# Opening of an attention and feed-forward kernel: weights in pairs, one more row from split parts, new orders on three engines

## The chip, the cores and the metric

The kernel runs on one core of one Trainium2 chip. Its engines are TensorE (PE; its weight loads are PEld), VectorE (DVE), ScalarE (ACT), GpSimd (POOL) and SyncE (SP), which issues the DMAs. The metric is the device time of one execution in microseconds (us), as the median of several runs.

## The reference

For 8 batches and 8 heads, x (512 tokens by 64) and a state (32 rows by 64) attend to each other; the 544 rows of a batch then pass through a feed-forward network of 512 to 2048 to 512.

```python
scores = scale * x @ state.T            # softmax over the 32 state rows
xread  = softmax(scores) @ state
scores2 = scale * state @ x.T           # softmax over the 512 tokens
sread  = softmax(scores2) @ x
rows = concat([xread, sread], axis=2)   # heads side by side: (8 * 544, 512)
h = rows @ w_in                         # 512 x 2048
g = h - tanh(h)
out = g @ w_out                         # 2048 x 512, float32
```

## The kernel before

The work goes in chunks: chunk i < 8 holds the 512 tokens of batch i, chunk 8 the 256 state rows of all batches. Instead of xread @ w_in, the kernel multiplies the attention weights a (tokens by 256 of head and state row) with m = state @ w_in, which it makes for each batch. A chunk takes 16 steps f, one for each 128 columns of the hidden layer: products into a PSUM bank (`hps`), tanh on ScalarE, the subtraction on VectorE, then the output products with row block f of w_out, summed over f in four banks. Operands are split into a high and a low part (a cast on ScalarE, a subtraction on VectorE), and three products (high x high, high x low, low x high) replace one in full precision. In the opening some products still take unsplit float32 operands; each such product is two instructions in the trace.

The weights come as 64-bit floats, 512 KB for each block of 128 rows or columns, and are turned into 32 bits by four steps: a shift on VectorE, a conversion of the low word on ScalarE, a carry on VectorE, an integer addition on VectorE.

**The opening** (steps 0 to 7 of chunk 0 and the hidden parts of steps 0 and 1 of chunk 1) is written out by hand as three lists, `lines`, one each for PE, DVE and ACT. Each engine runs its list strictly in that order. An entry is a letter and a number:

- a, r, b, p: the four steps (shift, conversion, carry, addition) of block j of w_in; p stores the block to `wf`. u, w, v, y: the same for block f of w_out; after y more loads are issued (`REFILL`). i, l: high and low part of that block.
- S, c, T, U: scores, their copy, their transposition. M, B, E, Z, I, J, N, A: maximum, subtraction, exp, sum, epsilon, reciprocal, scaling, transposition back: the first softmax, number 0 and 1 for batch 0, 2 and 3 for batch 1.
- m: block j of m for batches 0 and 1 (up to j = 3 for two batches more), from PE; k, R: copies to where PE reads it. e: more of them (j = 0, 1) for four batches. s, t, f, n: copies of e and m into tiles `e` and `f` that are stored to DRAM (`mearly`, `mlast`).
- P, d: high and low part of batch 0's attention; j, x: high and low part of block f of m (`fine`), for f of 4 and more. K, C: the same for batch 1.
- h, H: first and second half of the hidden products of step n (8 and 9 are chunk 1). X: tanh. L: subtraction. G, g: high and low part of the result, tile `g`. O, Q: output products for tokens 0 to 255 and 256 to 511. V: halves of chunk 0's output to DRAM.

`ops` and `more` state what each entry must follow. For f below `WHOLE_ROWS` the output products take the unsplit block and result. A tile belongs to a tag with a fixed count of buffers, and a new tile waits until all uses of the tile before it in that buffer are over. Tag `g` has three (`GB`), and the opening's tenants are in turn `head` (inputs of the first scores), the tiles e0 and e1, then the results g. DMAs are issued in order from SP's queue. All after the opening is ordered by a planner from estimates.

At the end, chunk 8 merges its three products: one matmul of 512 columns against the high weights gives high x high and high x low side by side in one bank, one of 256 adds low x high, and a copy on ScalarE (L480) and an addition on VectorE (L481) bring the halves together ahead of the tanh (L483).

Of the kernel before, what the change touches and what calls it, by code (L numbers as in the profile page):

```python
# [45 lines left out]
def attention_ffn(ctx: ExitStack, tc: tile.TileContext, early, xT, xn, bh, sm, sl, win, wout, xout, sout):  # L46
# [32 lines left out]
    wo = [cpool.tile([P, 2, DM], F32R, name=f"wo{f}") for f in range(NFF // 2)]  # L79
# [23 lines left out]
    def slots(name, shape, dtype):  # L103
        return pool.tile(shape, dtype, tag="slots", name=name, bufs=NFF // 2)
# [52 lines left out]


# [518 lines left out]
    def turn(j):  # L677
        es[j] = pool.tile([P, 512], F32, tag="e", name=f"e{j // 2}{j % 2}")
# [8 lines left out]
    def maximum(j):  # L687
        ms[j] = pool.tile([P, 16, 1], F32, tag="m1", name=f"m1{j // 2}{j % 2}")
        nc.vector.reduce_max(ms[j], e3(j), axis=AX.X)

    def sub_max(j):
        nc.vector.tensor_sub(e3(j), e3(j), ms[j].broadcast_to([P, 16, 32]))

    def exp(j):
        nc.scalar.activation(es[j], es[j], AF.Exp, scale=SCALE)

    def sums(j):
        if j < 2:
# [1 line left out]
        elif j == 2:  # L700
            z1.append(pool.tile([P, 2, 16, 1], F32, tag="z1", name="z1", bufs=1))
        if j > 1:
            zs[j] = z1[0][:, j - 2]
        nc.vector.reduce_sum(zs[j], e3(j), axis=AX.X)
# [9 lines left out]
    def normalize(j):  # L714
        nc.vector.tensor_mul(e3(j), e3(j), zs[j].broadcast_to([P, 16, 32]))
# [10 lines left out]
    def win_step(n):  # L726
        def run(j):
            if j not in csteps:
# [3 lines left out]
                csteps[j] = wcols[j].steps(wb[j // 2][:, j % 2], "cr")  # L732
            csteps[j][n]()
            if n == 3:
                nc.sync.dma_start(rows(wf[j // 4], j), wb[j // 2][:, j % 2].rearrange("p (r f) -> p r f", r=4))
        return run

    def wout_step(n):
        def run(f):
            if f not in wsteps:  # L740
                if f < WHOLE_ROWS:
                    if f % 2 == 0:
                        whole.append(pool.tile([P, 2, 512], F32, tag=("mr", "stage")[f // 2], name=f"wor{f}", bufs=(RRB, SB)[f // 2]))
                    worows[f] = whole[f // 2][:, f % 2]
                else:
                    worows[f] = pool.tile([P, 512], F32, tag="wor", name=f"wor{f}", bufs=RB)
                wsteps[f] = wos[f].steps(worows[f], "s")
            wsteps[f][n]()
            if n == 3:
                with ExitStack() as gates:  # L750
                    for x in stores:
                        gates.enter_context(tc.issue_after(x))
                    load(int(f in REFILL))
        return run

# [333 lines left out]
```

## Time and profile before

| | |
|---|---|
| median of 3 runs | 640.68 us (640.53 to 641.02) |
| profiled execution, its own time | 641.04 us |
| its span, first to last instruction | 639.3 us |
| PE busy | 631.6 us (99%), 3766 instructions |
| DVE busy | 440.0 us (69%) |
| ACT busy | 354.8 us (56%) |
| granted TensorE clock | 1.0 throughout |

Busy time is the sum of an engine's instructions. Since matmuls are pipelined and their ends are modelled, a row of a matmul may reach beyond the start of the next; the distance of starts is its cost in a stream. "idle before" in a row is the time that the engine stood still ahead of it, with what released it.

### The profile page before, as it was taken

What the parts mean: (1) busy time and instruction counts of PE and PEld (TensorE: products, weight loads), DVE (VectorE), ACT (ScalarE), POOL (GpSimd) and SP (SyncE); (2) the same over time, 40 slices, a digit from 0 to 9 for tenths busy, and PEclk for the clock granted to TensorE, in tenths of its full rate; (3) what the DMA queues carried; (4) which work ended last, traced back from release to release, by engine and by line L of the source; (5) the groups of instructions that cost most, each with busy time, mean ns of one, the idle gap of its engine ahead of it and who ended that gap; (6) DMA issues with size and microseconds to landing.
All of it is one profiled execution on the core that took longest, in us unless ns stands there. A gap on an engine that the chain in (4) does not pass through costs nothing.

```text
span 639.3 us, 10152 instructions
## 1 busy us (share of the span) xinstructions
PE 631.6 (99%) x3766; PEld 501.0 (78%) x3766; DVE 440.0 (69%) x775; ACT 354.8 (56%) x650; POOL 0.3 (0%) x5
## 2 busy tenths in 40 slices
PE   7999999999999999999999999999999999999997
PEld 4466866888888788878888788878888788888886
DVE  5999997798683874688563678396664875454663
ACT  4876677687783444656553458264543453343553
POOL 0000000000000000000000000000000000000000
PEclk9999999999999999999999999999999999999999
DMA  8994897477885335644533236772463024221410
GB/s 322 402 319 142 298 319 262 149 233 215 255 270 148 104 98 201 173 135 127 174 115 104 79 111 208 246 271 94 122 197 91 34 91 141 77 65 34 131 34 33
DMA packets 66592, 105.84 MB, mean 166 GB/s; under 512 B 12272, under 2 KB 32368, under 8 KB 66544
## 3 DMA queue, kind: packets, MB, share of 16 engines
q1 hardware_dynamic: 66544, 105.21, 50.7%
q8 instruction: 29, 0.48, 0.3%
q14 instruction: 19, 0.16, 0.1%
HBM read 69.01 MB, written 35.65 MB: 164 GB/s over the span
## 4 chain that ended last, share of the span: by engine, by line
PE 91%; DVE 5%; DMA 2%; ACT 1%; issue 0%; SPq 0%
PE ops L522 19%; PE ops L524 18%; PE ops L523 18%; PE hps L470 8%; PE hps L472 8%; PE hps L471 8%; PE hps L455 2%; PE mps L216 2%; PE rps L402 1%; PE hps L456 1%; DMA w00d<-in_win 1%; PE mps L215 1%; PE sps L284 1%; PE mps L766 1%; DVE w L150 1%; PE hps L828 1%
## 5 line engine op out<-in xcount | busy, mean ns | idle before, releaser
L522 PE MATMUL ops<-wo,g 128*128 128x512 f32 x534 | 209.3, 394 | 0.3 <-ACT g L116 0.3
L523 PE MATMUL ops<-wo,g 128*128 128x512 f32 x534 | 208.2, 390 | 0.0
L524 PE MATMUL ops<-wo,g 128*128 128x512 f32 x534 | 198.4, 390 | 0.0
L483 ACT ACTIVATE t<-hps 128x512 f32<-128x512 f32 x118 | 70.4, 598 | 148.4 <-PE hps L472 145.6
L483 DVE TENSOR_TENSOR t<-hps,t 128x512 f32<-128x512 f32 x118 | 81.0, 687 | 103.5 <-ACT t L483 103.2
L522 PEld LDWEIGHTS ops<-wo,g 128*128 128x128 f32 x534 | 100.3, 188 | 27.0 <-issue 3.0
L524 PEld LDWEIGHTS ops<-wo,g 128*128 128x128 f32 x534 | 100.0, 188 | 23.0 <-issue 1.7
L523 PEld LDWEIGHTS ops<-wo,g 128*128 128x128 f32 x534 | 100.3, 188 | 21.6 <-issue 1.6
L117 DVE TENSOR_TENSOR g<-t,g 128x512 fp32r<-128x512 f32 (+1 forms) x134 | 87.4, 656 | 32.7 <-ACT g L116 32.1
L116 ACT CAST g<-t 128x512 fp32r<-128x512 f32 (+1 forms) x134 | 79.6, 596 | 42.8 <-DVE t L483 36.8
L470 PE MATMUL hps<-aT,m 128*128 128x512 f32 x232 | 90.6, 391 | 0.0
L471 PE MATMUL hps<-aT,m 128*128 128x512 f32 x232 | 90.3, 389 | 0.0
L472 PE MATMUL hps<-aT,m 128*128 128x512 f32 x232 | 89.9, 390 | 0.0
L470 PEld LDWEIGHTS hps<-aT,m 128*128 128x128 f32 x232 | 43.5, 188 | 10.9 <-DVE t L483 1.1
L472 PEld LDWEIGHTS hps<-aT,m 128*128 128x128 f32 x232 | 43.6, 188 | 9.2
L471 PEld LDWEIGHTS hps<-aT,m 128*128 128x128 f32 x232 | 43.5, 188 | 8.9
L117 DVE TENSOR_TENSOR wst<-w,wst 64x512 fp32r<-64x512 f32 (+1 forms) x56 | 36.3, 648 | 7.2 <-ACT wst L116 5.5
L117 DVE TENSOR_TENSOR m<-mr,m 128x1024 fp32r<-128x1024 f32 x29 | 35.4, 1222 | 3.5 <-ACT m L116 3.0
L217 ACT COPY st<-mps 128x512 f32<-128x512 f32 (+1 forms) x56 | 29.7, 556 | 8.3 <-PE mps L216 5.2
L116 ACT CAST m<-mr 128x1024 fp32r<-128x1024 f32 x29 | 30.4, 1049 | 5.5 <-DVE mr L249 5.3
L116 ACT CAST wst<-w 64x512 fp32r<-64x512 f32 (+1 forms) x56 | 32.8, 586 | 0.7
L455 PE MATMUL hps<-srT,wm 128*128 128x512 f32 x64 | 23.1, 396 | 0.0
(251 smaller groups left out, 578.5 us busy)
## 6 DMA issues: line engine op xcount, KB each, us to landing
md<-st SPq DMA_DIRECT2D x96, 128.0 KB, 3.1
mr<-md SPq DMA_DIRECT2D x20, 512.0 KB, 4.3
xn<-in_xn SPq DMA_DIRECT2D x16, 512.0 KB, 6.0
out_x<-ob SPq DMA_DIRECT2D x30, 256.0 KB, 2.8
xT<-in_xT SPq DMA_DIRECT2D x12, 512.0 KB, 4.5
w<-wf SPq DMA_DIRECT2D x12, 512.0 KB, 5.0
pd<-pe SPq DMA_DIRECT2D x16, 256.0 KB, 2.1
p2t<-pd SPq DMA_DIRECT2D x64, 64.0 KB, 2.0
```

The source lines that it names most:

```text
L116: nc.scalar.copy(hi, src)
L117: return (sub or nc.vector).tensor_sub(lo, src, hi)
L216: nc.tensor.matmul(ps, s[:, 0, h], t[:, e], start=(g == 1), stop=True)
L217: nc.scalar.copy(stage[:, e], ps)
L455: nc.tensor.matmul(ps, mhi[k][:, cols], both, start=(k == 0), stop=False)
L470: nc.tensor.matmul(ps, mhi[k][:, cols], ahi[:, k], start=(k == 0), stop=False)
L471: nc.tensor.matmul(ps, mhi[k][:, cols], alo[:, k], start=False, stop=False)
L472: nc.tensor.matmul(ps, mlo[k][:, cols], ahi[:, k], start=False, stop=(k == 1))
L483: tanhs.append((nc.scalar.activation(t, ps, AF.Tanh).ins, nc.vector.tensor_sub(t, ps, t).ins))
L522: nc.tensor.matmul(o, g[:, 0, tok], wo[f][:, 0, cols], start=first, stop=False)
L523: nc.tensor.matmul(o, g[:, 0, tok], wo[f][:, 1, cols], start=False, stop=False)
L524: return nc.tensor.matmul(o, g[:, 1, tok], wo[f][:, 0, cols], start=False, stop=last).ins
```

## The change

- Blocks 4 and 5, 6 and 7 of w_in, and 0 and 1, 2 and 3, 4 and 5, 6 and 7 of w_out are loaded side by side into one tile (class `Pair`) and converted by one set of steps of 1,024 words, also i and l of w_out. Entries with the odd numbers vanish from the lists. The order of the 16 first loads, the buffers of the raw tiles and of the steps' temporaries, and the later loads' places (`REFILL`) change with it.
- The softmax of batch 1 (M, B, E, Z and K, C) runs over both halves in operations of 1,024 words, also the high and low part of its attention; transpositions and scaling stay separate.
- `WHOLE_ROWS` is 1: the output products of step 1 are made from high and low parts, with G1 and g1 new in the lists.
- The tiles f2 and f3 are two single ones on another tag.
- The lists are ordered anew; on PE, H3 comes ahead of O2.
- The last step of chunk 8 takes twelve products of 256 columns into one half of a bank, without the copy and the addition.

```diff
-REFILL = (0, 1, 2, 5, 6)
+REFILL = {0: 0, 2: 1, 4: 1, 6: 3}
 FINE = 4
-WHOLE_ROWS = 2
+WHOLE_ROWS = 1
...
-    wo = [cpool.tile([P, 2, DM], F32R, name=f"wo{f}") for f in range(NFF // 2)]
+    wop = [cpool.tile([P, 2, 2, DM], F32R, name=f"wo{f}") for f in range(0, NFF // 2, 2)]
+    wo = [wop[f // 2][:, f % 2] for f in range(NFF // 2)]
...
+    raws = itertools.chain(ring[:4], [twins], itertools.cycle([twins] * 2 + [parts] * PB))
...
+        pair, place, home = None, 0, None
+
         def load(self):
+            if self.home:
+                if self.pair.raw is None:
+                    words = self.src.dtype != F32
+                    shape = [P, 2, 512, 2] if words else [P, 2, 512]
+                    self.pair.raw = self.home(f"{self.name}d", shape, U32 if words else F32)
+                dst = self.pair.raw[:, self.place]
+                if len(dst.shape) > 2:
+                    dst = dst.rearrange("p f w -> p (f w)")
+                loadlog.append(nc.sync.dma_start(dst, self.src.bitcast(dst.dtype)).ins)
+                return
...
+    class Pair:
+        raw = None
+
+        def __init__(self, first, second, home):
+            self.src = first.src
+            for place, w in enumerate((first, second)):
+                w.pair, w.place, w.home = self, place, home
+
+        def steps(self, dst, r):
+            if self.src.dtype == F32:
+                return [lambda: None] * 3 + [lambda: nc.gpsimd.tensor_copy(dst, self.raw)]
+            low, high = self.raw[:, :, :, 0], self.raw[:, :, :, 1]
+            u, i = dst.bitcast(U32), dst.bitcast(I32)
+            top = self.raw.rearrange("p k f w -> p k (f w)").bitcast(U16).rearrange("p k (f w) -> p k f w", w=4)[:, :, :, 3]
+            carry = r.bitcast(U16).rearrange("p k (f w) -> p k f w", w=2)[:, :, :, 1]
+            return [
+                lambda: nc.vector.tensor_scalar(u, high, 3, 0x3FFFFFFF, ALU.logical_shift_left, ALU.bitwise_and),
+                lambda: nc.vector.tensor_scalar(carry, top, 0xC000, None, ALU.bitwise_and),
+                lambda: nc.scalar.activation(r, low, AF.Copy, scale=2.0**-29),
+                lambda: nc.vector.tensor_add(i, i, r),
...
+            if i == B and f == NFF - 1:
+                for k in range(4):
+                    for w, x in ((mhi, 0), (mhi, 1), (mlo, 0)):
+                        nc.tensor.matmul(
+                            ps[:, :n], w[k][:, cols], aTs[B][:, k, x], start=(k == 0 and w is mhi and x == 0),
+                            stop=(k == 3 and w is mlo),
+                        )
+                self.finish(f, ps[:, :n])
+                return
...
+                if f < NFF - 1:
+                    nc.scalar.copy(h, ps[:, n:])
+                    nc.vector.tensor_add(h, ps[:, :n], h)
+                    ps = h
...
-        wcols[:3] + wos[:1] + wcols[3:4] + wos[1:2] + wcols[4:5] + wos[2:3] + wcols[5:6]
-        + wos[3:4] + wcols[6:7] + wos[4:5] + wcols[7:8] + wos[5:8] + w0[2][0:2]
+        wcols[:3] + wos[:1] + wcols[3:4] + wos[1:2] + wcols[4:6] + wos[2:4] + wcols[6:8] + wos[4:8] + w0[2][0:2]
...
+    w_out_pairs = {
+        f: Pair(wos[f], wos[f + 1], other("aT0", 1) if f == 0 else slots if f < 6 else other("m", MB)) for f in (0, 2, 4, 6)
+    }
+    w_in_pairs = {j: Pair(wcols[j], wcols[j + 1], slots) for j in (4, 6)}
...
+            return e1[0].rearrange("p k (a n) -> p (k a) n", n=32)
...
+            e1.append(pool.tile([P, 2, 512], F32, tag="wf", name="e1", bufs=WB))
+        es[j] = e1[0][:, j - 2] if j > 1 else pool.tile([P, 512], F32, tag="e", name=f"e0{j}")
...
+        n = 16 if j < 2 else 32
+        ms[j] = pool.tile([P, n, 1], F32, tag="m1" if j < 2 else "m2p", name=f"m1{j // 2}{j % 2}", bufs=2 if j < 2 else 1)
...
+                if j < 4:
+                    csteps[j] = wcols[j].steps(wb[j // 2][:, j % 2], "cr")
+                else:
+                    csteps[j] = w_in_pairs[j].steps(wb[j // 2], parts(f"w0{j}r", [P, 2, 512], I32))
...
+                tag, bufs = ("mr", RRB) if f == 0 else ("stage", SB)
+                whole[f] = pool.tile([P, 2, 512], F32, tag=tag, name=f"wor{f}", bufs=bufs)
+                worows.update((f + x, whole[f][:, x]) for x in range(2))
+                wsteps[f] = w_out_pairs[f].steps(whole[f], (parts if f else twins)(f"wo{f}r", [P, 2, 512], I32))
...
-                    load(int(f in REFILL))
+                    load(REFILL[f])
...
-        nc.scalar.copy(wo[f][:, 0], worows[f])
+        nc.scalar.copy(wop[f // 2][:, :, 0], whole[f])
...
-                tag, bufs, n = ("ob", OB, 1) if j < 2 else ("stage", SB, 2)
-                t = pool.tile([P, n, 2, 2, P], F32, tag=tag, name=f"f{j}", bufs=bufs)
-                tiles.update((j + i, t[:, i]) for i in range(n))
+                tag, bufs = ("ob", OB) if j < 2 else ("wor", RB)
+                tiles[j] = pool.tile([P, 2, 2, P], F32, tag=tag, name=f"f{j}", bufs=bufs)
...
-            nc.scalar.copy(aTs[1][:, 0, j], ats[1][j])
+            nc.scalar.copy(aTs[1][:, 0], both[0])
...
-    more.update({"e1": "S2 s0 t0", "K0": "A2", "K1": "A3", "K2": "k3 R3"})
-    more.update({"I3": "Z2", "N2": "J3"})
+    more.update({"e1": "S2 s0 t0", "K0": "A2 A3", "K2": "k3 R3"})
+    more.update({"M2": "T3", "N3": "J2"})
...
-            more[f"O{n}"] = more.get(f"O{n}", "") + f" L{n} y{n}"
+            more[f"O{n}"] = more.get(f"O{n}", "") + f" L{n} y0"
         elif n < HALF:
-            more[f"O{n}"] = f"g{n} l{n}"
+            more[f"O{n}"] = f"g{n} l{n - n % 2}"
...
-    for j in range(2, 8):
-        more[f"r{j}"] = f"p{j - 2}"
-        more[f"w{j}"] = f"y{j - 2}"
-        if j - 2 >= WHOLE_ROWS:
-            more[f"u{j}"] = f"l{j - 2}"
-            more[f"w{j}"] += f" l{j - 2}"
+    more.update({"r2": "p0", "r3": "p1", "u6": "l2"})
...
-            "D0 D0 D0 S0 W0 D0 D0 D0 D0 S1 m0 e0 D0 m1 S2 h0 h1 H0 e1 H1 m2 O0 h2 Q0 m3 H2 O1 Q1 h3 m4 O2 H3 "
+            "D0 D0 D0 S0 W0 D0 D0 D0 D0 S1 m0 e0 D0 m1 S2 h0 h1 H0 e1 H1 m2 O0 h2 Q0 m3 H2 O1 Q1 h3 m4 H3 O2 "
             "Q2 h4 H4 m5 O3 Q3 h5 H5 m6 O4 Q4 h6 H6 m7 O5 Q5 h7 H7 O6 Q6 h8 h9 H8 O7 H9 Q7"
         ),
         "DVE": (
-            "T0 U0 M0 a0 B0 b0 p0 Z0 T1 a1 M1 b1 B1 I0 p1 J0 Z1 N0 I1 A0 J1 N1 A1 a2 b2 p2 u0 v0 y0 L0 a3 u1 b3 L1 "
-            "p3 a4 v1 b4 y1 p4 u2 a5 v2 y2 u3 b5 d0 v3 l2 p5 L2 y3 d1 g2 u4 T2 v4 y4 a7 l3 b7 p7 u5 a6 x4 l4 L3 u6 "
-            "g3 v5 L4 b6 y5 x5 p6 g4 l5 v6 L5 u7 y6 x6 g5 v7 l6 T3 M2 M3 B2 L6 B3 x7 Z2 g6 Z3 I3 y7 J3 N2 L7 A2 N3 "
-            "l7 A3 g7 C0 C1 C2 L8 g8 l0 L9 l1 g9"
+            "T0 U0 M0 a0 B0 b0 p0 Z0 T1 a1 M1 b1 B1 I0 p1 J0 Z1 N0 I1 A0 J1 N1 A1 a2 b2 p2 u0 v0 y0 L0 a3 b3 L1 "
+            "p3 a4 l0 g1 u2 b4 p4 v2 y2 L2 d0 l2 g2 d1 u4 T2 a6 v4 y4 x4 b6 L3 p6 g3 u6 L4 l4 x5 g4 v6 T3 M2 L5 B2 x6 g5 "
+            "y6 Z2 L6 I2 J2 x7 g6 l6 N2 A2 L7 N3 A3 g7 C0 C2 L8 g8 L9 g9"
         ),
         "ACT": (
-            "c0 r0 E0 r1 c1 R0 n0 k0 f0 E1 s0 t0 n1 R1 k1 f1 r2 c3 c2 w0 X0 r3 s1 t1 X1 w1 n2 k2 R2 f2 r4 w2 P0 r5 "
-            "w3 i2 P1 i0 X2 w4 G2 k3 R3 f3 n3 r7 i3 k4 R4 j4 i4 X3 r6 w5 i1 G3 w6 X4 k5 R5 j5 G4 i5 X5 w7 k6 R6 j6 "
-            "G5 i6 X6 k7 R7 j7 E2 G6 E3 X7 i7 G7 K0 K1 K2 X8 V1 G8 V0 X9 V3 V2 G9"
+            "c0 r0 E0 r1 c1 R0 n0 k0 f0 E1 s0 t0 n1 R1 k1 f1 r2 c3 c2 w0 X0 r3 s1 t1 X1 n2 k2 R2 f2 i0 G1 r4 w2 P0 P1 k3 "
+            "R3 f3 n3 X2 i2 G2 w4 k4 R4 j4 r6 X3 w6 G3 i4 X4 k5 R5 j5 G4 X5 k6 R6 j6 G5 E2 X6 k7 R7 j7 G6 i6 X7 "
+            "G7 K0 K2 X8 V1 G8 V0 X9 V3 V2 G9"
```

## Rows read from the trace of the kernel before

**Rows 1.** Waits of TensorE, first and last: waiting, releaser, us total, times, longest.
```profile
PE sps L659 <- DMA xT<-in_early: 1.7, 1, 1.7
...
PE ops L522 <- ACT g L116: 0.3, 1, 0.3
```

**Rows 2.** Timeline of TensorE to 60 us: start, us, what, count, idle before.
```profile
22.29 1.98 PE L854 MATMUL ops<-wor,t 128*128 128x512 f32 x4
...
28.83 3.60 PE L854 MATMUL ops<-wor,t 128*128 128x512 f32 x8
...
38.02 0.45 PE L825 MATMUL hps<-aT,fine 128*128 128x512 f32 x1
...
45.00 0.50 PE L522 MATMUL ops<-wo,g 128*128 128x512 f32 x1
...
47.85 0.39 PE L823 MATMUL hps<-aT,fine 128*128 128x512 f32 x1
...
57.61 2.92 PE L828 MATMUL hps<-at,mr 128*128 128x512 f32 x6 [0.62 <-DVE at L724]
```

**Rows 3.** Timeline of the last 12 us, around the last state row.
```profile
631.21 0.37 ACT L480 COPY t<-hps 128x256 f32<-128x256 f32 x1 [0.59 <-PE hps L456]
...
631.61 0.42 DVE L481 TENSOR_TENSOR t<-hps,t 128x256 f32<-128x256 f32 x1 [0.54 <-ACT t L480]
...
633.48 0.50 PE L522 MATMUL ops<-wo,g 128*128 128x512 f32 x1 [0.30 <-ACT g L116]
```

**Rows 4.** Busy time by stretch: us, PE, PEld, DVE, ACT, POOL, clock, DMA.
```profile
40.00:50.00 10.00, 10.00 (x101) 7.25 (x101) 9.78 (x20) 6.64 (x15) 0.00 (x0) 1.00 1.09 335
```

**Rows 5.** Groups by line: operations of 1,024 words; busy us, mean ns.
```profile
L117 DVE TENSOR_TENSOR m<-mr,m 128x1024 fp32r<-128x1024 f32 x29 | 35.4, 1222 | 3.5 <-ACT m L116 3.0
...
L116 ACT CAST m<-mr 128x1024 fp32r<-128x1024 f32 x29 | 30.4, 1049 | 5.5 <-DVE mr L249 5.3
```

**Rows 6.** Timeline of VectorE to 75 us.
```profile
19.22 0.42 DVE L146 TENSOR_SCALAR wor<-wo0d 128x512 uint32<-128x512 uint32 x1
19.56 0.46 DVE L147 TENSOR_SCALAR wo0r<-wo0d 128x512 uint16<-128x512 uint16 x1
20.06 0.69 DVE L150 CUSTOM_DVE_ANT_0 wor<-wor,wo0r 128x1024 uint16<-128x1024 uint16 x1
...
37.50 0.42 DVE L881 TENSOR_TENSOR fine<-mr,fine 128x256 fp32r<-128x256 f32 x1
...
66.17 0.42 DVE L146 TENSOR_SCALAR wor<-wo8d 128x512 uint32<-128x512 uint32 x1
```

**Rows 7.** Timeline of ScalarE to 75 us: a conversion, and casts G2 and G4.
```profile
18.13 0.72 ACT L149 ACTIVATE wo0r<-wo0d 128x512 int32<-128x512 uint32 x1
...
31.07 0.62 ACT L841 CAST g<-t 128x512 fp32r<-128x512 f32 x1 [0.70 <-DVE t L836]
...
42.28 0.62 ACT L841 CAST g<-t 128x512 fp32r<-128x512 f32 x1 [0.47 <-DMA mearly<-e]
```

**Rows 8.** Timeline of SyncE's DMA issues: start, us.
```profile
11.45 0.33 SPq L133 DMA_DIRECT2D wo1d<-in_wout  x1
```

**Rows 9.** DMA issues by line: count, KB each, us to landing.
```profile
wo1d<-in_wout SPq DMA_DIRECT2D x1, 512.0 KB, 9.0
```

**Rows 10.** Line L813, 31.5 to 33.5 us: durations, starts, then landing.
```profile
L813 SPq DMA_DIRECT2D mearly<-e x2: 1083/1358/1633, 30.7 to 31.9; - x2
...
DMA to landing us min/median/max: 4.9/5.1/5.3
```

**Rows 11.** Timeline of narrow products near the end.
```profile
629.32 0.28 PE L456 MATMUL hps<-srT,wm 128*128 128x256 f32 x1
...
629.44 0.40 PE L455 MATMUL hps<-srT,wm 128*128 128x512 f32 x1
...
635.33 0.27 PE L523 MATMUL late<-wo,g 128*128 128x160 f32 x1
635.44 0.27 PE L524 MATMUL late<-wo,g 128*128 128x160 f32 x1
```

More of the change, by code (lines that the diff above doesn't have):

```diff
@@ L103, in slots @@
     def slots(name, shape, dtype):
-        return pool.tile(shape, dtype, tag="slots", name=name, bufs=NFF // 2)
+        return pool.tile(shape, dtype, tag="slots", name=name, bufs=NFF // 4)
     ring = [parts] * PB + [twins] * 2
@@ L273, in convert_wout @@
         part.convert(w)
-        if f >= NFF // 2:
-            wo.append(slots(f"wo{f}", [P, 2, DM], F32R))
+        if f >= NFF // 2 and f % 2 == 0:
+            both_rows = slots(f"wo{f}", [P, 2, 2, DM], F32R)
+            wo.extend([both_rows[:, 0], both_rows[:, 1]])
         split(wo[f][:, 0], wo[f][:, 1], w)
@@ L635, in attention_ffn @@
     csteps, wsteps = {}, {}
+    e1 = []
     tanhs = []
     late = []
-    both, whole, halves, z1, fine = [], [], [], [], {}
+    both, whole, halves, z1, fine = [], {}, [], [], {}
     def rows_of(j):
@@ L677, in turn @@
     def turn(j):
-        es[j] = pool.tile([P, 512], F32, tag="e", name=f"e{j // 2}{j % 2}")
+        if j == 2:
+            e1.append(pool.tile([P, 2, 512], F32, tag="wf", name="e1", bufs=WB))
+        es[j] = e1[0][:, j - 2] if j > 1 else pool.tile([P, 512], F32, tag="e", name=f"e0{j}")
         if j == 0:
@@ L687, in maximum @@
     def maximum(j):
-        ms[j] = pool.tile([P, 16, 1], F32, tag="m1", name=f"m1{j // 2}{j % 2}")
+        n = 16 if j < 2 else 32
+        ms[j] = pool.tile([P, n, 1], F32, tag="m1" if j < 2 else "m2p", name=f"m1{j // 2}{j % 2}", bufs=2 if j < 2 else 1)
         nc.vector.reduce_max(ms[j], e3(j), axis=AX.X)
     def sub_max(j):
-        nc.vector.tensor_sub(e3(j), e3(j), ms[j].broadcast_to([P, 16, 32]))
+        nc.vector.tensor_sub(e3(j), e3(j), ms[j].broadcast_to([P, 16 if j < 2 else 32, 32]))
     def exp(j):
-        nc.scalar.activation(es[j], es[j], AF.Exp, scale=SCALE)
+        e = es[j] if j < 2 else e1[0].rearrange("p k x -> p (k x)")
+        nc.scalar.activation(e, e, AF.Exp, scale=SCALE)
     def sums(j):
@@ L699, in sums @@
             zs[j] = pool.tile([P, 16, 1], F32, tag="z", name=f"z0{j}")
[L700 to L704, printed above, removed]
+        else:
+            z1.append(pool.tile([P, 32, 1], F32, tag="z1", name="z1", bufs=1))
+            zs.update((2 + x, z1[0][:, 16 * x : 16 * x + 16]) for x in range(2))
+        nc.vector.reduce_sum(zs[j] if j < 2 else z1[0], e3(j), axis=AX.X)
     def add_eps(j):
@@ L714, in normalize @@
     def normalize(j):
-        nc.vector.tensor_mul(e3(j), e3(j), zs[j].broadcast_to([P, 16, 32]))
+        e = es[j].rearrange("p (a n) -> p a n", n=32)
+        nc.vector.tensor_mul(e, e, zs[j].broadcast_to([P, 16, 32]))
     def turn_back(j):
@@ L731, in run @@
                     wb[j // 2] = pool.tile([P, 2, 512], F32, tag=tag, name=f"w00{j}", bufs=bufs)
-                csteps[j] = wcols[j].steps(wb[j // 2][:, j % 2], "cr")
+                if j < 4:
+                    csteps[j] = wcols[j].steps(wb[j // 2][:, j % 2], "cr")
+                else:
+                    csteps[j] = w_in_pairs[j].steps(wb[j // 2], parts(f"w0{j}r", [P, 2, 512], I32))
             csteps[j][n]()
             if n == 3:
-                nc.sync.dma_start(rows(wf[j // 4], j), wb[j // 2][:, j % 2].rearrange("p (r f) -> p r f", r=4))
+                for x in (j,) if j < 4 else (j, j + 1):
+                    nc.sync.dma_start(rows(wf[x // 4], x), wb[x // 2][:, x % 2].rearrange("p (r f) -> p r f", r=4))
         return run
@@ L740, in run @@
             if f not in wsteps:
[L741 to L747, printed above, removed]
+                tag, bufs = ("mr", RRB) if f == 0 else ("stage", SB)
+                whole[f] = pool.tile([P, 2, 512], F32, tag=tag, name=f"wor{f}", bufs=bufs)
+                worows.update((f + x, whole[f][:, x]) for x in range(2))
+                wsteps[f] = w_out_pairs[f].steps(whole[f], (parts if f else twins)(f"wo{f}r", [P, 2, 512], I32))
             wsteps[f][n]()
@@ L884, in low_part @@
         if j < 2:
-            nc.vector.tensor_sub(aTs[1][:, 1, j], ats[1][j], aTs[1][:, 0, j])
+            nc.vector.tensor_sub(aTs[1][:, 1], both[0], aTs[1][:, 0])
         else:
@@ L955, in ready @@
         fn, before = ops[x[0]]
-        need = [c + x[1:] for c in before if not (c + x[1:] in SKIP)] + more.get(x, "").split()
-        return all(y in done for y in need)
-    SKIP = {"S3", "J2",  "k8", "k9", "R8", "R9"}
+        need = [c + x[1:] for c in before] + more.get(x, "").split()
+        return all(y in done or y in given for y in need)
+    given = {"S3", "J3", "k8", "k9", "R8", "R9"}
     with tc.manual_schedule(engines={mybir.EngineType.PE, mybir.EngineType.DVE, mybir.EngineType.Activation}):
@@ L967, in attention_ffn @@
                     done.add(x)
+                    if x[0] in "abrp" and int(x[1:]) > 3:
+                        done.add(f"{x[0]}{int(x[1:]) + 1}")
                     moved = True
```

10 lines of the change are left out of this document (3 added, 7 removed).

## Prediction

> **What bounds the kernel now.** I read the waits of TensorE first, then the busy time by stretch, then the orders of TensorE, VectorE and ScalarE up to 66 us side by side, then the SyncE queue, then the last 12 us. The waits of TensorE are six entries, the last two of 0.3 us [rows 1]: after 15 us it stands idle only before h8 (0.62 us) and near the end (0.30 us) [rows 2, 3]. So TensorE sets the time, any wait that the change puts into its order is lost for good, and at most about a microsecond of idle is left to win after the first 15 us. In the opening VectorE is as full: 9.78 of 10 us, where ScalarE has 6.64 [rows 4]. An engine with 2% to spare cannot catch up after it has been held. The 16 first weights come in one after another at the pace of the DMA queue, so what is late there is late for everyone.
>
> **How I worked.** I walked the three written orders: every operation starts when its engine has finished the one ahead, and when its operands, its buffer and its load are there; durations are those of the rows. Walked so from 17 us on, the orders of before put h8 at 57.6 us; the row has 57.61 [rows 2]. The walk of the new orders, with the same durations, gives the terms below.
>
> Durations of operations of 1,024 words stand in rows of two other lines: a subtraction on VectorE 1.22 us, a cast on ScalarE 1.05 us [rows 5], against 0.69 and 0.62 for 512 [rows 6, 7]. From one start to the next that is about 1.13 instead of 2 x 0.60, and 0.95 instead of 2 x 0.52. For the shift u (0.42 for 512 [rows 6]) and the carry v (0.46) no row has 1,024; between no growth and doubling I take 0.60 and 0.65 from start to start, since their slope is about half that of the subtraction. ScalarE's w (0.72 [rows 7]) becomes 1.13.
>
> **Part 1: pairs.** Six pairs save VectorE about 0.22 us each (three fixed parts of some 0.07), four low parts 0.07 each, the second softmax and the low part of the second chunk's attention another 0.3: together 1.9 us. ScalarE saves 0.1 per joined operation. None of this is on TensorE. What it costs is a start: both rows must have landed. Row 1 of w_out is issued at 11.45 [rows 8] and lands 9.0 us later [rows 9], at 20.45. Before, u0 began at 19.22 [rows 6] with row 0 alone. Now w0 runs 20.48 to 21.6 on ScalarE, v0 21.6 to 22.3, y0 to 23.5, and L0, which stands behind y0 in VectorE's order, to 24.2; X0, its tanh, stands behind w0 on ScalarE and ends at 22.1, in time. O0 needs both and starts at 24.25; before it started at 22.29 [rows 2]. **TensorE waits 2.1 us** by the walk. If the pair were converted as fast as one row it would still wait about 1.2; the ends are 1.2 and 2.5.
>
> **Part 2: row 1 from high and low parts.** Eight full-precision instructions took 3.60 us (O1 and Q1); twelve products of split rows took 45.00 to 47.85, 2.85 us [rows 2], some 3.0 with the same overhang at the end. **TensorE gains 0.6 us.** But f=1 now needs a tile g. The tag g has three buffers, and their first tenants are the head of the inputs, and the tiles e0 and e1 that are stored to mearly. Before, g2 took the first, g3 the second, g4 the third: G4 at 42.28 waited for the store of e1, the only such wait [rows 7], and G2 at 31.07 did not. Now g1 takes the first and G2 must wait for the stores of e0. These are issued at 30.7 and 31.9 and take 4.9 to 5.3 us [rows 10]: landed at 36.8. Nothing ahead of them in SyncE's order changes (same loads, same sends), so they are no earlier. G2 ends at 37.45, O2 starts then. TensorE, though O0 was late, is there at 35.9, since H3 now stands before O2: **it waits 1.6 us, and 0.25 more for g2**. Behind G2 on ScalarE stand w4, k4, R4, j4, r6; behind g2 on VectorE everything.
>
> **Part 3: the order behind g2.** From 37.5 VectorE does g2, d1, u4, T2, a6, v4, y4, x4: 0.60, 0.60, 0.60, 0.63, 0.60, 0.76 (with a short wait for itself), 1.13, 0.42, so x4 is there at 42.85. Before, x4 ran at 37.50 [rows 6] and the product that reads it at 38.02 [rows 2]. Now O2 and Q2 end at 40.5, two products of h4 follow, and the third **waits 1.9 us**. TensorE is 4.8 us late there. From then on VectorE and TensorE keep nearly the same pace: waits of 0.2 and 0.6 in O3 (p6, 1.13 us long, stands before g3), 0.2 before h6 and 0.3 in O6, but none before h8, whose softmax row is now out in time.
>
> The sum up to the end of the opening: new waits 2.1 + 1.9 + 1.9 + 1.3 = 7.2 us, less 1.5 that the same walk has in the orders of before (0.8 of it before h8), less 0.6 to 0.8 for part 2: 4.9 to 5.1. The walk itself has h8 at 62.5 and Q7 4.9 us later than before; I take **+4.9**. Ends: 2.5 if G2 found its buffer free, 6.1 if the stores landed 1.2 us later.
>
> [...]
>
> **Part 4: loads and buffers.** The refills of SyncE move: w20 behind y2 and w21 behind y4, about where they were, and wo8, w22, w23 behind y6, now at about 55. Their users come from 66 us on (wo8's first shift at 66.17 [rows 6]), some 5 us later now; a load takes about 5 us, so this is hidden. wo8 shares the two buffers of w20 and w21 and can be loaded only after w20 is converted, so it lands near 76; its products come eight steps later. I take 0; it may cost up to 3 us if VectorE stands in order before it (second rival). The tiles f2 and f3 on another tag and the pairs' raw tiles lie in buffers without a tenant: 0.
>
> **Part 5: the last state row.** Before, the hidden row 15 went through a copy (631.21) and an addition (631.61) ahead of its tanh; TensorE then waited 0.30 us for its g at 633.48 [rows 3]. Without the two the chain is 0.86 us shorter, more than the wait: **-0.3**. Next is TensorE's own work. Price: twelve products of 256 columns instead of four of 512 and four of 256. One of 256 took 0.12 (629.32 to 629.44), and 160 columns, each with its weights, 0.11 [rows 11]: 12 x 0.12 = 1.44 against 4 x (0.24 + 0.12) = 1.44. I take 0; at the worst, if each took the 0.24 of 512 columns, 1.4 would be added, less what the next wait takes up.
>
> **Sum.** 641.04 (the profiled execution: span 639.3) + 4.9 - 0.3 = 645.64. That execution lay 0.36 above the median of the runs shown, so against it: **645.3**.
>
> **Rivals.**
> - *G2 doesn't wait* (the buffer is assigned otherwise, or e0's stores land before 34). For it: the order of tenants is only inferred from G4's wait. Against it: that wait fits no other order. Then only the late O0 and VectorE's order count: the walk gives +2.6, with the end 643.0.
> - *More is lost later*: wo8 waits behind w20 and VectorE, 9.8 of 10 us busy, stands before its conversion; or G2 gets the buffer of e1, free only near 41. Price 2 to 4.6 more: 647.5 to 650. Against it: nothing of chunk 1 needs wo8 for eight steps.
> - *The grouping pays and the loads are early enough*, the other side: VectorE's 1.9 us put L0, g2 and x4 in time, O0 moves by less than TensorE's order can take up. Then 0.6 + 0.6 (h8) + 0.3 are won: 639.2. It decides from the landing of row 1: it would have to be under 18.5 us instead of 20.45, and e0's stores before 34. Both landings stand in rows of before, and the queue ahead of them is the same.
> - *The late opening is taken up*: if the gain in VectorE's work let h4 and O3 run through, the waits of parts 1 to 3 would shrink to about the 1.5 that go: 640.7, no change.
>
> **Chances.** Forecast 0.59, G2 free 0.13, more lost 0.08, grouping pays 0.12, no change 0.08. Under about 0.2% (1.3 us) this kernel's measurement cannot tell a change from none. Faster 0.12, same 0.08, slower 0.80. The likeliest case alone spans 644 to 647 (landing of e0's stores +-1 us, waits in O3 to O6). The range reaches from the upper part of no change to the start of "more lost": 640.9 to 648.5.
>
> [...]
>
> **What would show it.** In the profile after: O0 (the first output products) near 24.2, released by VectorE; ScalarE idle for about 3 us before the cast of g2, released by the store to mearly, at about 37; VectorE idle 1.2 us near 19.3 and 2.4 us before g2; the third product of h4 near 42.8; no wait before h8; near the end no idle before the last row's first product. Wrong would be: g2 cast before 35, or a span up to h8 under 59 us.

## The result, and the profile after

The changed kernel takes **645.25 us** (median of 5 runs, 644.84 to 646.84, one disturbed run left out) against 640.37 us before on the same chip: a ratio of 1.0069 (95% interval 1.0049 to 1.009), **slower** by 0.7%. The profiled execution took 645.30 us with a span of 643.5. The prediction had 645.3 and, for the profiled execution, 645.64.

The waits of TensorE come first (waiting, releaser, us in total, times, longest). Two new ones have taken their places behind the opening's load [rows 1]: O0 waits for L0 (L891), and O2 for the cast G2 (L896). The wait of 0.3 us near the end is gone.

```profile
PE sps L710 <- DMA xT<-in_early: 2.1, 1, 2.1
PE ops L909 <- DVE t L891: 1.6, 1, 1.6
PE ops L566 <- ACT g L896: 1.6, 1, 1.6
...
PE ops L568 <- DVE g L900: 0.3, 1, 0.3
```

The timeline of TensorE (start, us, what, count, idle before) shows the same places as [rows 2]: O0, the begin of O2, two products of Q2, the second and third product of h4, and h8. O0 comes 1.78 us later than before, the third product 5.02 (38.02 before), h8 5.21.

```profile
24.07 1.98 PE L909 MATMUL ops<-wor,t 128*128 128x512 f32 x4 [1.62 <-DVE t L891]
...
37.65 0.50 PE L566 MATMUL ops<-wo,g 128*128 128x512 f32 x1 [1.60 <-ACT g L896]
...
40.29 0.63 PE L568 MATMUL ops<-wo,g 128*128 128x512 f32 x1
40.72 0.63 PE L566 MATMUL ops<-wo,g 128*128 128x512 f32 x1
...
42.42 0.56 PE L879 MATMUL hps<-aT,fine 128*128 128x512 f32 x1
43.04 0.50 PE L880 MATMUL hps<-aT,fine 128*128 128x512 f32 x1
...
62.82 2.73 PE L883 MATMUL hps<-at,mr 128*128 128x512 f32 x6
```

On ScalarE's timeline the conversion of the pair's low words, w0, waits for the landing of the second row, and the cast G2, 31.07 before [rows 7], stands for 3.15 us behind the store to mearly:

```profile
20.16 1.16 ACT L188 ACTIVATE wo0r<-wo0d 128x1024 int32<-128x1024 uint32 x1 [1.80 <-DMA wo0d<-in_wout]
...
36.98 0.62 ACT L896 CAST g<-t 128x512 fp32r<-128x512 f32 x1 [3.15 <-DMA mearly<-e]
```

VectorE's timeline has the three conversions of the first pair (shift, carry, addition), then g2, which waits 2.54 us for G2, and x4, which releases the third product of h4:

```profile
20.18 0.70 DVE L186 TENSOR_SCALAR wor<-wo0d 128x1024 uint32<-128x1024 uint32 x1 [0.80 <-DMA wo0d<-in_wout]
21.35 0.80 DVE L187 TENSOR_SCALAR wo0r<-wo0d 128x1024 uint16<-128x1024 uint16 x1 [0.48 <-ACT wo0r L188]
22.18 1.23 DVE L189 CUSTOM_DVE_ANT_0 wor<-wor,wo0r 128x2048 uint16<-128x2048 uint16 x1
...
37.63 0.69 DVE L900 TENSOR_TENSOR g<-t,g 128x512 fp32r<-128x512 f32 x1 [2.54 <-ACT g L896]
...
42.57 0.42 DVE L936 TENSOR_TENSOR fine<-mr,fine 128x256 fp32r<-128x256 f32 x1
```

By stretch (columns as in [rows 4]), VectorE was the full engine that had to stand idle, 7.42 of 10 us from 30 to 40, and ran without a gap behind it:

```profile
30.00:40.00 10.00, 8.40 (x58) 4.95 (x57) 7.42 (x10) 5.51 (x12) 0.00 (x0) 0.97 1.05 311
40.00:50.00 10.00, 9.51 (x70) 6.25 (x76) 9.96 (x16) 5.77 (x10) 0.00 (x0) 0.86 1.05 326
50.00:60.00 10.00, 10.00 (x101) 7.41 (x101) 9.67 (x14) 6.56 (x13) 0.00 (x0) 1.00 0.23 79
```

Near the end, the answer to [rows 3]: the last state row's products (x5 is the end of the twelve), its tanh straight from the accumulator, the first output product of the row without idle time, and the last product.

```profile
635.47 0.74 PE L489 MATMUL hps<-srT,wm 128*128 128x256 f32 x5
...
636.31 0.39 ACT L527 ACTIVATE t<-hps 128x256 f32<-128x256 f32 x1 [0.62 <-PE hps L489]
...
638.11 0.39 PE L566 MATMUL ops<-wo,g 128*128 128x512 f32 x1
...
640.28 0.27 PE L568 MATMUL late<-wo,g 128*128 128x160 f32 x1
```

Before, the last product stood here:

```profile
635.77 0.28 PE L524 MATMUL late<-wo,g 128*128 128x160 f32 x1
```

**Where the time went.** Both kernels run the same tanh activations in the same order (144 on ScalarE), so their starts can be laid side by side. From 60 to 588 us, 98 of 121 are 5.05 us late in the changed kernel, within 0.06, from the first to the last (the others moved singly): all of the loss is made before h8, nothing is lost or won in the long middle. The last product is 4.51 late (640.28 less 635.77), so the tail gives 0.54 back. The rest, down to the 4.2 by which the spans differ (643.5 and 639.3), lies behind the last product. "Behind" in the table below is this lag against the kernel before, at 384 us.

### The profile page after: what moved, and what is told of

Its sections match the earlier page's. It is cut to its first block, busy times and chain, and to the rows that moved or that the text cites. A ratio compares the mean times of both kernels' runs of the same rounds, so it can differ in the third digit from the quotient of the medians.

```text
span 643.5 us, 10129 instructions
## 1 busy us (share of the span) xinstructions
PE 633.0 (98%) x3774; PEld 502.8 (78%) x3774; DVE 438.5 (68%) x749; ACT 353.7 (55%) x638; POOL 0.3 (0%) x5
## 4 chain that ended last, share of the span: by engine, by line
PE 92%; DMA 3%; DVE 2%; ACT 1%; issue 1%; SPq 0%; ACTq 0%
PE ops L566 19%; PE ops L568 19%; PE ops L567 19%; PE hps L513 8%; PE hps L514 8%; PE hps L515 8%; PE hps L498 2%; PE mps L249 2%; DMA wo0d<-in_wout 1%; DMA w01d<-in_win 1%; PE rps L436 1%; PE hps L499 1%; PE mps L248 1%; PE sps L318 1%; PE mps L822 1%
## 5 line engine op out<-in xcount | busy, mean ns | idle before, releaser
L527 ACT ACTIVATE t<-hps 128x512 f32<-128x512 f32 (+1 forms) x119 | 71.1, 597 | 145.8 <-PE hps L515 142.6
L527 DVE TENSOR_TENSOR t<-hps,t 128x512 f32<-128x512 f32 (+1 forms) x119 | 81.3, 684 | 99.7 <-ACT t L527 99.2
L498 PE MATMUL hps<-srT,wm 128*128 128x512 f32 x60 | 21.7, 396 | 0.0
```

Of the source, the lines that this page charges most:

```text
L498: nc.tensor.matmul(ps, mhi[k][:, cols], both, start=(k == 0), stop=False)
L527: tanhs.append((nc.scalar.activation(t, ps, AF.Tanh).ins, nc.vector.tensor_sub(t, ps, t).ins))
```

## The experiments

| kernel | median (runs), us | before there | h0 | O0 | h8 | h0 to h8 | behind, us |
|---|---|---|---|---|---|---|---|
| before | 640.37 (6) | | 16.34 | 22.29 | 57.61 | 41.27 | 0 |
| changed | 645.25 (5) | 640.37 | 16.42 | 24.07 | 62.82 | 46.40 | 5.05 |
| 1 own buffer for e0 | 644.15 (6) | 640.73 | 15.65 | 23.66 | 60.14 | 44.49 | 2.37 |
| 2 first pair's rows together | 644.97 (5) | 640.73 | 15.90 | 22.25 | 61.93 | 46.03 | 4.18 |
| 3 both | 643.44 (8) | 640.73 | 15.26 | 22.29 | 59.95 | 44.69 | 2.18 |
| 4 row 1 whole | 641.90 (12) | 640.94 | 16.32 | 23.89 | 59.13 | 42.81 | 1.36 |
| 5 row 1 whole, rows together | 640.62 (11) | 640.94 | 15.97 | 22.87 | 57.87 | 41.90 | 0.11 |
| 6 before, row 15 unmerged | 641.26 (11) | 640.73 | 16.38 | 22.32 | 57.63 | 41.25 | 0.02 |
| 7 before, other orders | 639.11 (11) | 640.94 | 16.01 | 21.96 | 56.02 | 40.01 | -1.65 |
| 8 as 1, once more | 643.09 (1) | 640.17 | 14.93 | 22.97 | 59.14 | 44.21 | 1.66 |
| 9 as 3, once more | 641.05 (1) | 640.17 | 15.01 | 21.61 | 58.42 | 43.41 | 0.65 |

The column h0 is the start of TensorE's first hidden product. It differs by up to 1.5 us between the profiles, because the inputs landed earlier in some: the first scores, which wait for them, started at 9.51 us before and at 8.80 in run 1. No edit changes what is loaded or runs ahead of the inputs. So "behind" and h8 hold some of this chance, and "h0 to h8" leaves most of it out. The rows of before and of run 1:

```profile
9.51 1.08 PE L659 MATMUL sps<-xT,head 128*64 128x512 f32 x4 [1.73 <-DMA xT<-in_early]
16.34 2.84 PE L828 MATMUL hps<-at,mr 128*128 128x512 f32 x6
```

```profile
8.80 1.08 PE L710 MATMUL sps<-xT,head 128*64 128x512 f32 x4 [1.15 <-DMA xT<-in_early]
15.65 2.84 PE L883 MATMUL hps<-at,mr 128*128 128x512 f32 x6
```

Theory: the chain of part 2 (buffer of e0, two more VectorE operations ahead of g2) and the late first pair of part 1 make the loss, one behind the other on VectorE. Rivals: the 1,024-word operations themselves; one of the two alone; the clock.

**1. A buffer of its own for e0.** This takes away what makes G2 wait.

```
-                tag, bufs = ("g", GB)
+                tag, bufs = ("g", GB) if j else ("mr13", 1)
```

> The changed kernel with one edit: tile e0 takes a buffer of its own (that of the w_in pair 6, unused until 40 us), so g2 finds a free buffer. Theory (VectorE's chain, held by the store of e0 and by the late pair): ScalarE no longer waits 3.15 us for mearly ahead of G2, O2 starts near 35.9 instead of 37.65, h8 near 60.1 instead of 62.8, and the time falls by 2.4 us, to 642.9 (+0.4% over before). Rival 1 (the operations of 1,024 words alone hold the order up): no change, 645.3. Rival 2 (only the wait for the first pair counts, what follows is absorbed): no change, 645.3. Rival 3 (TensorE's half clock between 39 and 42 us is what costs): the shorter wait keeps the clock up and 2.4 us or more are won, but only in executions whose clock was below 1.

Ratio to before 1.006 (1.0041 to 1.0079). The wait of O2 is gone, and one stands in its place that the changed kernel does not show as idle time: x4, now at 39.88, is still late for h4. TensorE's waits, then its timeline:

```profile
PE ops L909 <- DVE t L891: 2.0, 1, 2.0
PE hps L880 <- DVE fine L936: 1.5, 1, 1.5
...
PE sps L318 <- ACT st L250: 0.6, 1, 0.6
```

```profile
38.45 0.39 PE L879 MATMUL hps<-aT,fine 128*128 128x512 f32 x1
40.35 0.50 PE L880 MATMUL hps<-aT,fine 128*128 128x512 f32 x1 [1.52 <-DVE fine L936]
...
60.14 2.74 PE L883 MATMUL hps<-at,mr 128*128 128x512 f32 x6
```

"Behind" falls by 2.7 us (5.05 less 2.37), but 0.8 of that are the inputs; from h0 to h8 the edit is worth 1.9. In the time it is 1.5: 3.4 us above before instead of 4.9, where the theory's 642.9 was 2.5. From 394 to 417 us 1.15 us are lost again, where TensorE waits for a softmax (L318) whose chain stood behind a load, wn. Runs 8 and 9 come back to this.

**2. The first two rows of w_out loaded together**, ahead of the fourth column block.

```
-        wcols[:3] + wos[:1] + wcols[3:4] + wos[1:2] + wcols[4:6] + ...
+        wcols[:3] + wos[:2] + wcols[3:6] + ...
```

> The changed kernel with one edit: row 1 of w_out is loaded ahead of block 3 of w_in, so that the first pair is complete 1.3 us earlier. Theory: O0 starts near 22.9 instead of 24.07, but G2 still waits for the store of e0, O2 still starts at 37.6, and the time stays at 645.3 (within 0.3). Rival 2 (the late first pair is what costs): 1.3 us less, 644.0. Rival 1: no change.

Ratio 1.0068 (1.0056 to 1.008). O0 starts 1.82 us earlier (0.5 of it with the inputs), and the timeline of TensorE shows its wait moved to O2:

```profile
22.25 1.98 PE L909 MATMUL ops<-wor,t 128*128 128x512 f32 x4 [0.33 <-DVE t L891]
...
36.71 0.79 PE L566 MATMUL ops<-wo,g 128*128 128x512 f32 x1 [2.48 <-ACT g L896]
```

1.62 + 1.60 has become 0.33 + 2.48. The 0.9 us that remain of the gain in this profile are the stores of e0, which came 0.9 earlier; the medians show 0.3 (645.25 to 644.97; against the kernel before beside them 0.6) and the ratios next to nothing. Here the wait that ends on these stores took up the rest of what was won ahead of it (1.60 us became 2.48).

**3. Both edits.**

> Both edits: e0 in a buffer of its own, and row 1 of w_out loaded ahead of block 3 of w_in. Theory: 2.8 us less than the changed kernel, 642.5, that is 0.4 less than with the buffer alone; what is then left over before (2.1 us, +0.33%) is VectorE's work for row 1's split parts, which stands ahead of the rest. Rival 1: no change, 645.3. Rival 2: 1.3 less, 644.0.

Ratio 1.0045 (1.003 to 1.0061): 643.44 us, 0.9 above the theory (0.6 when both are reckoned from the kernel before beside them). O0 waits 1.0 and h4's third product 2.4 us: the opening is still 2.2 us behind. But e0's new buffer is not free of others either: the w_in pair 6 takes it next, and VectorE, which now comes to that pair's shift (a6) earlier than the 40 us of the expectation, waits there for the same store. The row is VectorE's:

```profile
36.91 0.69 DVE L186 TENSOR_SCALAR w<-w06d 128x1024 uint32<-128x1024 uint32 x1 [1.22 <-DMA mearly<-e]
```

Three operations behind it stands x4, for which h4 waits. In run 1 this wait was 0.23 us, in run 9 0.56, in run 8 none. So run 3 doesn't show what is left once the store is out of the way; the 1,024-word operations and VectorE's two extra operations remain possible beside it. This profile was the slowest of its runs: 4.0 us were lost at 415 to 430 us.

**4. Row 1 of w_out whole again.** No g1, no G1, and l0 and i0 at the end of their orders; pairs stay.

```
-WHOLE_ROWS = 1
+WHOLE_ROWS = 2
-  "p3 a4 l0 g1 u2 b4 ...   ... C0 C2 L8 g8 L9 g9"
+  "p3 a4 u2 b4 ...         ... C0 C2 L8 g8 l0 L9 g9"
-  "... R2 f2 i0 G1 r4 w2 ...   G7 K0 K2 X8 ..."
+  "... R2 f2 r4 w2 ...         G7 K0 K2 i0 X8 ..."
```

> The changed kernel with row 1 of w_out taken whole again, as before (two full-precision products per instruction pair, no g1 and G1, and the low part l0 and the shift i0 at the end of their orders); pairs, loads and the last state row stay as changed. Computes all of it. Theory: part 2 alone costs 3.6 us of the 5.0 that the opening lost, since it takes a buffer of tag g (G2 then waits for the stores of e0) and puts 1.7 us of VectorE's work (l0, g1) ahead of g2. So no wait for G2, O0 still waits some 2 us for L0 near 24.2, h8 starts at 59.0 (changed kernel 62.82, before 57.61), and the time is 641.0 to 642.0 (changed kernel 645.2 less 3.6). Rival 1, the operations of 1,024 words alone make the loss (a pair starts late and VectorE cannot catch up), and row 1 does not matter: h8 stays above 61.5, time 644 to 645.5. Rival 2, only the buffer mattered, not VectorE's work: the same as with e0 in a buffer of its own, h8 near 60.1, time 642.7 to 644.

Ratio 1.0024 (1.0001 to 1.0046). h8 at 59.13, time 641.9: the theory's 59.0 and 641.0 to 642.0, where one rival wanted more than 61.5. From the other, that only the buffer mattered, it is told by the stretch from O0 to h8: 35.24 us here, 35.32 before, 36.48 in run 1, and 36.17 in run 8, where nothing waits for the store. So the work of the split row (l0 and g1 on VectorE, i0 and G1 on ScalarE) costs some 0.9 us beyond what its cheaper products give back, as far as one profile of each can tell. The time is 1.0 us above before instead of 4.9, so part 2 as a whole makes **3.9 us** of the loss (expected 3.6). How it divides between the buffer and VectorE's work, no run shows in the time (run 1's 1.5 us for the buffer are net of its loss around 410 us).

**5. The same, and the first two rows together.**

> The same, and the first two rows of w_out loaded one behind the other, ahead of the fourth column block of w_in. Computes all of it. Theory: with the buffer, VectorE's two operations and the late first pair all gone, nothing of the opening's loss is left: O0 waits under 1.2 us, h8 at 57.3 to 58.0 (before 57.61), and with the last state row unmerged the time is 640.0 to 640.9, the same as before within 0.1%. So the pairs themselves gain nothing, although they take 1.9 us of work from VectorE: TensorE had only 0.6 us to win before h8. Rival 1, the 1,024-word pairs cost by themselves: h8 above 59, time over 642. Rival 2, the pairs pay once they are not late: h8 below 57, time under 639.7.

Ratio 0.9993 (0.9982 to 1.0005). In the time nothing of the loss is left, with all pairs in place (from h0 to h8 it is 0.6 us more than before): x4 is ready before h4 asks for it, on TensorE's timeline the third product (38.56) follows the second without a gap, and the waits left are O0's 0.9 and 0.2 in O3.

```profile
22.87 1.99 PE L909 MATMUL ops<-wor,t 128*128 128x512 f32 x4 [0.89 <-DVE t L891]
...
38.34 0.39 PE L879 MATMUL hps<-aT,fine 128*128 128x512 f32 x1
38.56 0.39 PE L880 MATMUL hps<-aT,fine 128*128 128x512 f32 x1
...
57.87 2.74 PE L883 MATMUL hps<-at,mr 128*128 128x512 f32 x6
```

Against run 4 the load order is worth 1.3 us (641.90 to 640.62), where in run 2, with G2's wait behind it, it showed 0.3 to 0.6. The rival of the 1,024-word operations falls. So does the other: in these orders the pairs win nothing by themselves. A search for orders like that of run 7 was not made for the pairs.

**6. The kernel before, with only the last state row unmerged** (the two blocks of the diff at its end).

> The kernel before with one part of the change alone: the last hidden row of the state chunk in twelve products of 256 columns, without copy and addition. Theory: the wait of 0.30 us before the last row's first output product goes, and the slower restart after it (0.34 instead of 0.23 us to the next product): 0.3 to 0.6 us less, 640.4 to 639.9 (-0.07%). Rival (narrow products bound by their weight loads): 0.5 us more or no change.

Ratio 1.0003 (0.9994 to 1.0012): no difference that can be measured. In the profile TensorE's wait for g is gone, and the last row goes from the first of its products to the last of the output in 6.11 us (629.36 to 635.47) instead of 6.67, but 0.26 of it was lost ahead of the row. The last late product is 0.30 earlier, but the span is 0.3 longer (639.6 and 639.3): in this profile what lies behind the last product took the gain. The theory's 0.3 to 0.6 us are not shown.

**7. The kernel before, row 15 unmerged, other orders of VectorE and ScalarE in the opening.** Same operations of 512 words; 63 of 114 places of VectorE's order differ. Some of the moves:

```
-  ... b2 p2 u0 v0 y0 L0 a3 u1 b3 L1 p3 a4 v1 b4 y1 ...   l6 T3 M2 M3 B2 L6 B3 x7 Z2 g6 ...
+  ... b2 u0 p2 v0 L0 y0 a3 b3 v1 u1 p3 a4 u2 L1 y1 b4 ...   y4 b7 x4 M2 a7 u5 L3 T3 v5 g3 ... B2 L5 M3 x6 B3 ...
```

> The kernel before, with the last state row unmerged as in the changed kernel, and new written orders for VectorE and ScalarE in the opening: same operations of 512 words, some moved past each other, found by the walk of the orders. Computes all of it. Theory: before h8 the old orders leave 0.6 to 0.8 us of TensorE idle (the softmax row of the second chunk is late), which is all that an order can win; with the row unmerged 0.3 more: h8 at 56.1 by the walk (56.9 if only the idle time of the rows can go), time 0.7 to 1.8 us below the kernel before, 638.9 to 640.0. Rival, the opening is bound by TensorE's own work and by loads, and what the order gains before h8 is lost at the next wait: h8 57.3 to 57.9, time 640.2 to 641.

**639.11 us**, ratio 0.9978 (0.9959 to 0.9997): it beats both kernels, against before by 1.8 us in the medians, with an interval from 0.2 to 2.6 us. h8 is at 56.02, where the walk of the orders has 56.1; 0.3 of that nearness is luck, since the inputs came so much earlier than in the profile of before, and from h0 to h8 1.26 us are won. TensorE's idle time is gone from all four stretches from 20 to 60 us (first and last of them):

```profile
20.00:30.00 10.00, 10.00 (x146) 4.96 (x146) 9.93 (x23) 9.60 (x22) 0.00 (x0) 1.00 1.03 408
...
50.00:60.00 10.00, 10.00 (x41) 7.25 (x40) 9.90 (x19) 5.58 (x11) 0.00 (x0) 1.00 0.36 129
```

**8 and 9. Runs 1 and 3 once more**, one execution each and on another chip, for the loss around 410 us.

> One more look at the kernel with e0 in a buffer of its own, unchanged; computes all of it. In its first trace 1.15 us of the 2.7 us won in the opening were lost again between 394 and 417 us, where a softmax waited for a load. Theory: this loss comes from how late transfers are there in one execution, not from the order of the work; then the gain over the changed kernel from 60 to 384 us is 2.7 us again within 0.2, and the loss at 394 to 430 us is another (0 to 4 us). Rival: it belongs to this order, since the opening ends earlier against the transfers; then 1.1 to 1.2 us are lost again at the same place.

> One more look at the kernel with both edits (e0 in a buffer of its own, first two rows of w_out one behind the other), unchanged; computes all of it. In its first trace 4.0 us were lost between 415 and 430 us. Theory as for the run beside it: the gain of 2.9 us over the changed kernel from 60 to 384 us comes again, the loss behind it is another, time 642 to 646. Rival: 3.9 to 4.1 us are lost again at the same place.

Run 8: 643.09 us, 1.66 behind at 384 us, and 1.1 lost again at the same place. Run 9: 641.05 us, 0.65 behind, and nothing lost. The gains in the opening that both theories wanted again (2.7 and 2.9 us over the changed kernel) came out at 3.4 and 4.4. On ScalarE's timeline the cast that waits for wn, in run 3 and in run 9:

```profile
421.18 0.62 ACT L115 CAST wm<-wn 128x512 fp32r<-128x512 f32 x1 [6.17 <-DMA wn<-wf]
```

```profile
416.35 0.62 ACT L115 CAST wm<-wn 128x512 fp32r<-128x512 f32 x1 [2.87 <-DMA wn<-wf]
```

The same program, 4.0 us lost once and none the other time: that loss comes with the transfers of one execution. In run 3 wn landed 8.25 us after its issue (412.91 to 421.16), in run 9 5.51. Run 1 is another case, since it lost the same 1.1 twice, as the rival says. There the load took 5.3 and 5.2 us, but it was issued late: ahead of it on SyncE stand eight issues (L450), which took 8.31 us in run 1 and 8.41 in run 8, against 6.47 in the changed kernel.

```profile
404.91 8.31 SPq L450 DMA_DIRECT2D sr<-sx  x8
...
414.75 0.38 SPq L290 DMA_DIRECT2D wn<-wf  x1
```

Whether an order that ends its opening earlier meets this more often stays open, but it is no simple rule: of the ten profiles beside that of before, those of runs 1, 3, 4 and 8, 1.4 to 2.4 us behind at 384 us, lose between 0.3 and 4.0 there, and the six that were further behind or further ahead lose nothing.

The opening itself also differs between executions: run 8 was 1.0 us earlier than run 1, run 9 1.5 us earlier than run 3, of which the inputs make 0.7 and 0.3. So single profiles of the opening differ by up to 1.5 us, from h0 to h8 by 0.3 and 1.3. The sizes in the time rest on medians.

## Why the prediction was right

| step | forecast | measured |
|---|---|---|
| w0 starts, released by the landing of row 1 | 20.48 | 20.16 |
| O0 starts; waits | 24.25; 2.1 | 24.07; 1.62 |
| G2 ends | 37.45 | 37.60 |
| O2 waits | 1.6 | 1.60 |
| third product of h4 | 42.85 | 43.04 |
| h8 | 62.5 | 62.82 |
| opening | +4.9 | +5.05 |
| last row | -0.3 | -0.54 (run 6: no change in the time) |

The inputs came alike in the two profiles that are compared here (h0 at 16.34 and 16.42 us), so this agreement owes them nothing.

**Part 1.** Mechanism and size held; runs 2 and 5 show both sides of it (0.3 and 1.3 us of time). Of the unknown durations the shift came as taken (0.60 from start to start, 38.84 to 39.44); the carry took 0.64, and 0.78 to 0.83 where the addition that reads it comes next (taken: 0.65 and 0.76). O0's wait was 0.5 shorter than forecast. L0 and O0 were 0.2 earlier. The other 0.3 is a matter of counting: the profile counts idle time from the modelled end of the products ahead (22.45), whereas before O0 started ahead of that end, and all TensorE work ahead of it came only 0.08 later than before.

**Part 2.** The order of the buffer's tenants was only inferred from the wait of G4, and it was right: runs 1 and 4 remove the wait in two different ways. The rival that G2 doesn't wait would have given 643.0; runs 1 and 8, in which it doesn't, took 644.15 and 643.09. The gain of 0.6 us from three products instead of two full ones came (from the second half of step 2 to the end of Q1 3.73 us, 29.64 to 33.37, before 4.39), but is in none of the ends: behind it stood G2.

**Part 3.** x4 set the pace as written, but the forecast wait of 1.9 us is not a wait in the profile. The granted clock was 0.50 from 39.4 to 42.5, eight products (39.44 to 42.42) ran 0.43 apart instead of 0.23, which makes 1.6 us, and the third product of h4 followed 0.05 behind x4. Run 1 shows the same place with the clock at full speed: there it is idle time, 1.52 us. Whoever had read the slow clock as the cause would have been wrong; executions of the changed kernel with a clock of 1.000 took 644.84 to 645.19.

**Part 4.** Held: wo8's conversion waited 0.38 us on VectorE at 75.19, TensorE did not.

**Part 5.** The profile gave 0.54 instead of 0.3: without the idle time the first products behind it also ran at their pace (638.11 to 638.34, where before the first stood 0.34 ahead of the second). Run 6 does not show this in the time.

**Rivals.** "The grouping pays" needed the second row under 18.5 us and e0's stores before 34. In run 5 G2 waits for no store, and the second row is there at 18.99 (w0 starts); the time is still the same as before within its interval. O0 waits 0.9 us in it, so what pairs would do with the row under 18.5 isn't tested. One sentence of the forecast was too narrow: that at most about a microsecond of idle was left to win after 15 us. Run 7 wins 1.8 in the medians by order, on the 512-word operations (with row 15 unmerged, which run 6 does not show in the time). From O0 to h8 it takes 34.06 us where before took 35.32. Of these 1.26, 0.77 lie in the last 8 us ahead of h8 (the listed 0.62, and the part of the wait that the modelled end of the product ahead covers), and 0.49 in h4, m4 and O3, where single products of before stood 0.29 to 0.39 apart instead of 0.23 without being listed as idle. The walk, which had 1.5 us of waits in the old orders, was nearer than the list of waits.

VectorE's own time did fall by the grouping (an addition of 1,024 words starts 1.15 us before the next operation, 22.18 to 23.33, against 2 x 0.60 for two of 512); run 5 shows no gain from it in the time (ratio 0.9993). In the changed kernel VectorE was busy for 9.28 of 10 us from 20 to 30, and the pair's later start still left TensorE idle for 1.62 us at O0.

## What to carry to other kernels

Before two operations are joined, look when the later of their two inputs lands: here the joined shift, released by that landing, started at 20.18 us, 0.96 later than the single one before, and what the pairs won in busy time on VectorE did not show in the time (run 5: ratio 0.9993). When an edit gives a buffer tag one tenant more, list all tenants in order: here G2, pushed onto a buffer that a DMA still read, waited 3.15 us for that store, and g2 and O2 behind it 2.54 and 1.60. Moving the stored tile elsewhere handed a wait to the next tenant there (a6 in run 3, 1.22 us). Before reading microseconds off single profiles, compare when their inputs landed (here up to 1.5 us apart). Where several waits follow each other on one engine, take the last one away first: run 2 shows what an earlier one is worth alone (0.3 to 0.6 us), run 5 what it is worth when the last is gone (1.3).

## What was not expected of the hardware

TensorE's granted clock fell to 0.50 shortly after the wait for G2: the engine had been idle from 36.05 to 37.65 us, ran at 0.99 from 37.6 to 39.4, at 0.50 to 42.5, and at 0.96 from there to 46, as the rows by stretch (columns as above) say:

```profile
36.00:37.60 1.60, 0.04 (x1) 0.00 (x0) 0.00 (x0) 0.62 (x2) 0.00 (x0) 1.00 1.11 327
37.60:39.40 1.80, 1.75 (x6) 1.16 (x7) 1.77 (x3) 1.77 (x4) 0.00 (x0) 0.99 1.12 327
39.40:42.50 3.10, 3.10 (x9) 2.32 (x7) 3.06 (x5) 2.84 (x4) 0.00 (x0) 0.50 1.02 293
42.50:46.00 3.50, 3.01 (x40) 1.37 (x38) 3.50 (x7) 1.75 (x3) 0.00 (x0) 0.96 1.10 339
```

Here this cost nothing, because the next operand was late anyway. In run 3 the clock fell as well, after the wait of 2.44 us for x4 and a few products at 1.00:

```profile
41.50:44.50 3.00, 3.00 (x30) 1.92 (x13) 3.00 (x5) 2.97 (x7) 0.00 (x0) 0.50 1.11 346
```

There the stretch from the third product of h4 to the first of h5 took 6.16 us (39.91 to 46.07) against 5.38 in run 9, which kept its clock; at h8 0.2 of these 0.8 us were left. A wait came ahead of each of these falls, also in run 2 (2.48 us at O2, then 0.50 from 37.6 to 39.4), but not every wait was followed by one: runs 8 and 9 stood still for 2.03 and 1.79 us at a stretch with the clock at 1.00. So the runs don't show what makes it fall.

Runs 3 and 9 showed the other surprise: the same load, wn, let its cast wait 6.17 us in one execution and 2.87 in another of the same program, 350 us behind the change.
